# Three layers in split precision: when sums of weights are asked for, which engine makes their low words, and where a plain pair of blocks stands

## The chip, the cores and the metric

The kernel runs on one core of a Trainium2 chip. A core has TensorE (matrix products, PE in the rows, with PEld for its loads of the stationary operand), VectorE (DVE), ScalarE (ACT), GpSimd (POOL) and SyncE (SP, which only issues transfers here). The metric is the device time of one execution in microseconds (us), lower is better. Products accumulate in PSUM banks; all other tiles lie in SBUF. GpSimd reads and writes SBUF only in this kernel.

## The reference, cut to what matters

Attention with a window and block summaries comes first (batch 2, 8 heads, 768 positions, 64 per head); its output is a matrix x of 1536 tokens by 512. Then:

```
h = np.maximum(np.maximum(x @ w1, x @ w2), x @ w3)   # 512 -> 768, layer 1
y = h @ w_out                                        # 768 -> 512, layer 2
out = (y @ w_a) * (y @ w_b) @ w_out2                 # 512 -> 1536 -> 512, layers 3 and 4
```

The diff touches layer 1 for the second half of the tokens.

## The kernel before, in words

**Precision.** A float32 operand is kept as two parts: a high word (ScalarE copies it to the rounded type) and a low word (the operand minus the high word). A product of two operands is three matmuls: high by high, low by high, high by low (`mm3`, L532). `w_parts` (L464, L465) makes the two words of a weight, `split` (L536, L537) those of an activation `hg`; the low word's engine is an argument of both.

**Tokens and blocks.** The tokens are four chunks of 384 columns, c = 0 to 3. Layer 1 has six output blocks f, each with three weights m (w1, w2, w3) of which the maximum is taken. Chunks 0 and 1 are done by `layers12` while the attention of chunks 2 and 3 still runs. Chunks 2 and 3 are done together by `pair1`, the function of the diff.

**Plain and fast pairs.** `pair1` takes two blocks f and f+1 with the same m as a 2x2 matrix problem: two blocks by two chunks. The order of these nine pairs is (0,0), (0,1), (0,2), (2,0), and so on to (4,2), where the first number is f and the second is m. A plain pair (`plain`) is 4 steps of 12 matmuls 128x384. A fast pair needs 7 products instead of 8 (`products`, table PRODUCTS): 7 steps of 6 matmuls, since a product of the table covers half of the contraction. `products` takes two fast pairs in turn, u = 0 and 1, so one turn has 14 steps. Products 0, 3 and 6 need the weights as they are; products 1, 2, 4 and 5 need sums of weights (S1 to S4), and most need sums of x (T1 to T4, made by `x_sums`).

**Sums of weights.** `w_sums` (from L609) makes them for one pair: GpSimd adds high and low words back to float32 (`rc`, two instructions 128x512, L614), VectorE makes four sums 128x256 (`s`, L471 to L474), ScalarE makes two high words (`wt<-s`, L464), and VectorE two low words (`wt<-s`, L465). Their buffers are the tag `ws`, of which WS are allowed. They are asked for at the steps WSUMS among the plain pairs, and within `products` behind products 2 and 5 of u = 1.

**Results.** `result` takes a finished product to float32 `pt` (ScalarE L638 for the first m of a plain pair, VectorE L640 or L633 and L635 for the others, which also take the maximum). When three values of m are seen, `split` makes the block's `hg`: ScalarE its high word, GpSimd its low word (VectorE for the last two blocks of chunk 3).

**Order.** The order of instructions on each engine is set when the program is built, from the dependencies and a timeline that the scheduler computes; TensorE may so run products of a later step first. Two things bind it by hand: `flush` delays the results of a step until the next step's matmuls are written, and `behind_marks` puts what is written in it behind the last marked instruction of its own engine: `mark[0]` on VectorE, `mark[1]` on ScalarE, `mark[2]` on GpSimd (the last `split` there).

**What surrounds it.** `layer2` multiplies the six `hg` of a chunk with w_out (`py`), 72 matmuls for a chunk; it comes after all pairs for chunks 2 and 3. At each step of `pair1` the loop at the end calls `weights(1)`, which brings weights of layers 3 and 4: SyncE issues the load (L434), ScalarE and VectorE take the 64-bit words apart (L454, L456, L458, L459), GpSimd adds the two halves (`w<-w`, int32, L460), then sums and words as above. `fits` lets them on only while no more than ROOM places are held beyond those freed (`w_freed`), and the first three of these loads wait for a small copy of a finished `hg` (`gate`, L433). SUMS names the steps at which sums of y for chunks 0 and 1 (batch 0) are made (`sums_of`, L742 to L747).

Of the kernel before, what the change touches and what calls it, by code (L numbers as in the profile page):

```python
# [19 lines left out]
P = 128  # L20
# [16 lines left out]
NCH, MAXT = len(CHUNKS), max(SIZES)  # L37
# [5 lines left out]
N1, N2, NK = 3 * FF1 // P, FF1 // P, FF2 // P // 3  # L43
# [9 lines left out]

W64, W32, WBUFS, QB, FB, SM, GB, BANKS = (6, 3), (4, 3), (24, 10), 4, (8, 1), 2, (12, 9), (2, 2, 1, 2, 2)

GATE, ROOM, SUMS, EARLY34 = (2, 1), 14, (40, 44, 48, 52), 6
PLAIN, XSUMS, WSUMS, WS, PT, MAX_G, LO_G = 3, (3, 5), (8, 10), 7, 7, False, False
RING, LEAD, TURN, ERA0, ASKS, AHEAD, PRE, TURNS = 8, 5, (11, 2, 4), 8, (3, 4, 5, 7, 9), (4, 1), 3, ((6, N1 - 6, 6, 4, 4), (24, 34), (34, 43))

# [10 lines left out]
def attention_then_maxout_then_bilinear(ctx: ExitStack, tc: tile.TileContext, qt, kt, vt, vwin, wall, const, out):  # L78
# [66 lines left out]
    @contextmanager  # L145
    def behind_marks():

        with ExitStack() as pins:
            for ins in mark + [marks.get(("normal", len(groups) - 1))]:
                if ins is not None:  # L150
                    pins.enter_context(tc.issue_after(ins))
            yield
# [362 lines left out]
    def flush():  # L515
        while late:
            late.pop(0)()

    def bank(name):

        return ps_m.tile([P, 512], F32, tag="m", name=name)

    def ring(name):
        return ps_m.tile([P, 512], F32, tag="r", name=name, bufs=RING)[:, 0:MAXT * P]
# [4 lines left out]
    def mm3(ps, w, o, x, first, last, more=False):  # L529

        for n, (i, j) in enumerate(((0, 0), (1, 0), (0, 1))):
            ins = T.matmul(ps, w[:, i, o:o + P], x[:, j], start=first and n == 0, stop=last and n == 2, skip_group_check=more).ins  # L532
        return ins

    def split(dst, src, eng):
        A.activation(dst[:, 0], src, AF.Copy)  # L536
        ins = eng.tensor_tensor(dst[:, 1], src, dst[:, 0], ALU.subtract).ins  # L537
        if eng is G:
            mark[2] = ins
# [44 lines left out]
    def x_sums(k):  # L584

        if not xs:
            both_x = x_p.tile([P, 4, 2, 2, MAXT * P], F32R, tag="xs", name="xs", bufs=1)
            xs.update({f"T{j + 1}": both_x[:, j] for j in range(4)})

        def whole(c, k):  # L590
            t = y_p.tile([P, MAXT * P], F32, tag="xr", name="xr", bufs=4)
            G.tensor_tensor(t, x_t[c, k][:, 0], x_t[c, k][:, 1], ALU.add)
            return t

        def diff(name, x, y):
            t = y_p.tile([P, MAXT * P], F32, tag="xd" + name, name="xd", bufs=1)
            V.tensor_tensor(t, x, y, ALU.subtract)
            A.activation(xs[name][:, 0, k], t, AF.Copy)
            V.tensor_tensor(xs[name][:, 1, k], t, xs[name][:, 0, k], ALU.subtract)
            return t  # L600

        b11, b12 = whole(2, k), whole(3, k)
        t1 = diff("T1", b12, b11)
        b22, b21 = whole(3, 2 + k), whole(2, 2 + k)
        t2 = diff("T2", b22, t1)
        diff("T3", b22, b12)
        diff("T4", b21, t2)

    def w_sums(f, m):  # L609

        w0, w1 = (w_t[3 * (f + i) + m] for i in range(2))
        r0, r1 = (w32_p.tile([P, 512], F32, tag="rc", name="rc", bufs=2) for _ in range(2))
        for r, w in ((r0, w0), (r1, w1)):
            G.tensor_tensor(r, w[:, 0], w[:, 1], ALU.add)  # L614
        s12, s34 = sums4(*(r[:, o:o + 256] for r in (r0, r1) for o in (0, 256)))
        eng = G if LO_G else V
        s12, s34 = (w_parts(x, eng, "ws") for x in (s12, s34))
        w_s[f, m] = {"A11": (w0, 0), "A12": (w0, 256), "A22": (w1, 256),
                     "S1": (s12, 0), "S2": (s12, 256), "S3": (s34, 0), "S4": (s34, 256)}
# [3 lines left out]
    def pair1():  # L623

        nonlocal w_freed
        part, seen, hs = {}, {}, {2: {}, 3: {}}

        def result(f, c, to, x=None):

            prev, t = part.get((f, c)), half("pt")  # L630
            part[f, c] = t
            if x is not None:
                mark[0] = V.tensor_tensor(t, to, x, ALU.add).ins  # L633
                if prev is not None:
                    ins = (G if MAX_G else V).tensor_tensor(t, t, prev, ALU.max).ins  # L635
                    mark[2 if MAX_G else 0] = ins
            elif prev is None:
                mark[1] = A.activation(t, to, AF.Copy).ins  # L638
            else:
                mark[0] = V.tensor_tensor(t, to, prev, ALU.max).ins  # L640
            seen[f, c] = seen.get((f, c), 0) + 1
            if seen[f, c] == 3:
                hs[c][f] = h = hg_p.tile([P, 2, MAXT * P], F32R, tag="hg", name="hg")
                split(h, t, V if f >= N2 - 2 and c == 3 else G)
                if c == GATE[0] and f == GATE[1]:
                    gate.append(h[:, 0, 0:1])

        def plain(f, m):

            nonlocal w_freed  # L650
            for c in (2, 3):
                for i in range(2):
                    ps = bank("ph")[:, 0:MAXT * P]
                    for k in range(4):
                        mm3(ps, w_t[3 * (f + i) + m], k * P, x_t[c, k], k == 0, k == 3)
                    flush()
                    late.append(lambda f=f + i, c=c, ps=ps: result(f, c, ps))
                    yield
            w_freed += 2

        def operand(name, k):
            if name in xs:
                return xs[name][:, :, k]
            return x_t[1 + int(name[2]), 2 * (int(name[1]) - 1) + k]

        def products(two, ahead):

            nonlocal w_freed
            ps, kept = {}, {}
            for i in range(7):  # L670
                for u, (f, m) in enumerate(two):
                    w, y, name = PRODUCTS[i]
                    first = (u, name) not in ps
                    if first:
                        ps[u, name] = ring(f"h{name}")
                    (wt, o), to = w_s[f, m][w], ps[u, name]
                    for k in range(2):
                        mm3(to, wt, o + k * P, operand(y, k), first and k == 0, k == 1, not first)
                    flush()

                    def evac(i=i, u=u, f=f, to=to):
                        if i < 3:
                            kept[u, i] = t = half(("s1", "m5", "u2")[i])
                            mark[1] = A.activation(t, to, AF.Copy).ins
                        elif i == 3:
                            result(f, 2, to, kept[u, 0])
                        elif i == 4:
                            result(f + 1, 3, to, kept[u, 1])
                        elif i == 5:
                            result(f, 3, to, kept[u, 2])  # L690
                        else:
                            result(f + 1, 2, to)

                    late.append(evac)
                    if (i, u) in ((2, 1), (5, 1)) and ahead:
                        with behind_marks():
                            w_sums(*ahead.pop(0))
                    yield
            w_freed += 2 * len(two)

        order = [(f, m) for f in range(0, N2, 2) for m in range(3)]
        fast = order[PLAIN:]
        ahead, step = fast[:], 0
        for f, m in order[:PLAIN]:
            for _ in plain(f, m):
                step += 1
                with behind_marks():
                    if step in XSUMS:
                        x_sums(XSUMS.index(step))
                    elif step in WSUMS:  # L710
                        w_sums(*ahead.pop(0))
                yield
        while len(fast) - len(ahead) < 2:
            with behind_marks():
                w_sums(*ahead.pop(0))
        for j in range(0, len(fast), 2):
            yield from products(fast[j:j + 2], ahead)
        for c in (2, 3):
            yield from layer2(c, hs[c], ring)
        w_freed += N2  # L720
# [43 lines left out]
    def half(tag):  # L764
        return mo_p.tile([P, MAXT * P], F32, tag=tag, name=tag, bufs={"ca": 9, "t": 3, "pt": PT}.get(tag, 2))
# [138 lines left out]
    for i, _ in enumerate(pair1()):  # L904
        with behind_marks():
            weights(1)
            if i in SUMS:
                m = SUMS.index(i)
# [60 lines left out]
```

## Time and profile before

| | before |
|---|---|
| median of three runs | 562.57 us (562.47 to 563.86) |
| the profiled execution | 563.56 us, its span 561.8 us |
| TensorE busy | 539.5 us (96% of the span) |
| VectorE busy | 422.7 us (75%) |
| ScalarE busy | 283.1 us (50%) |
| GpSimd busy | 237.9 us (42%) |
| mean granted TensorE clock | 0.991 |

Durations in the rows are those of the profiled execution, and times count from the start of its span; 1.76 us of its time lie outside the span. The granted clock is given as a share of 2.4 GHz. `x12` is a count of instructions, `out<-in` names the tiles. Where a row ends in brackets, the engine sat idle before it for that time, and the arrow names what ended the idle time. Idle time of an engine costs nothing by itself: it counts where TensorE, which has the most work, waits at the end of the chain.

### The profile page before, as it was taken

The numbers are of one execution on the slowest core, as the hardware profiler recorded it, in microseconds if no ns is written. First come the engines' busy times: TensorE is split into PE (matmuls) and PEld (weight loads), VectorE is DVE, ScalarE is ACT, GpSimd is POOL, SyncE is SP. The second block draws the span as 40 slices with busy tenths as digits, with TensorE's granted clock in tenths as the row PEclk, the third lists the DMA queues.
The fourth block names the chain that finished last, engine by engine and source line by source line (L and its number), as shares of the span: only waits on it lengthen the run. The fifth ranks groups of instructions, "written<-read, shape, count | busy, mean of one in ns | idle before, by whom it ended". The sixth has DMA issues, their size and how long they took to land.

```text
span 561.8 us, 9048 instructions
## 1 busy us (share of the span) xinstructions
PE 539.5 (96%) x3328; PEld 510.8 (91%) x3328; DVE 422.7 (75%) x875; ACT 283.1 (50%) x692; POOL 237.9 (42%) x195
## 2 busy tenths in 40 slices
PE   7899999999999999797999899999999999999997
PEld 7789999999999999796999878988998998998986
DVE  4798976875445569589899898797797798584464
ACT  4699765766533334364866553544552653340130
POOL 3479997642144263544426523521441252140130
PEclk9999999999999999889999999999999999999999
DMA  8994534383000000131131232222123111000015
GB/s 302 359 299 163 190 114 146 120 272 108 22 1 2 1 0 1 56 129 48 70 112 49 104 113 82 69 76 75 39 76 113 39 50 63 0 1 2 0 39 187
DMA packets 17132, 51.82 MB, mean 92 GB/s; under 512 B 2112, under 2 KB 2752, under 8 KB 17088
## 3 DMA queue, kind: packets, MB, share of 16 engines
q1 hardware_dynamic: 17088, 51.25, 27.2%
q8 instruction: 26, 0.43, 0.3%
q14 instruction: 18, 0.15, 0.1%
HBM read 48.09 MB, written 3.15 MB: 91 GB/s over the span
## 4 chain that ended last, share of the span: by engine, by line
PE 74%; DVE 14%; POOL 4%; ACT 3%; DMA 2%; issue 1%; SPq 1%; POOLq 0%; ACTq 0%; DVEq 0%
PE ph L532 18%; PE qb L532 12%; PE py L532 8%; PE qg L532 6%; PE po L841 5%; PE po L840 5%; PE po L842 5%; PE qd L532 3%; PE ps L261 3%; PE hb L532 3%; DVE wt L465 3%; PE psv L318 2%; POOL w L460 2%; PE pst L299 2%; DVE w L459 1%
## 5 line engine op out<-in xcount | busy, mean ns | idle before, releaser
L460 POOL TENSOR_TENSOR w<-w,w 128x512 int32<-128x512 int32 x60 | 94.0, 1573 | 137.1 <-DVE w L459 84.6
L532 PE MATMUL qb<-yt,wt 128*128 128x384 f32 x576 | 109.3, 335 | 0.3 <-ACT s L791 0.3
L532 PE MATMUL ph<-x,wt 128*128 128x384 f32 x576 | 106.8, 339 | 0.0
L532 PEld LDWEIGHTS qb<-yt,wt 128*128 128x128 f32 x576 | 100.9, 188 | 1.6 <-ACT s L791 0.6
L532 PEld LDWEIGHTS ph<-x,wt 128*128 128x128 f32 x576 | 99.2, 188 | 0.3
L808 POOL TENSOR_TENSOR t<-t,ca 128x384 f32<-128x384 f32 x36 | 44.0, 1236 | 68.9 <-DVE t L807 68.8
L532 PE MATMUL py<-hg,wt 128*128 128x384 f32 x288 | 56.6, 347 | 4.1 <-ACT hg L536 4.1
L532 PE MATMUL qg<-yt,wt 128*128 128x384 f32 x288 | 57.5, 335 | 1.0 <-DVE acc L852 1.0
L842 PE MATMUL po<-wt,hg 128*128 128x512 f32 (+1 forms) x146 | 56.7, 388 | 1.5 <-DVE hg L537 1.5
L840 PE MATMUL po<-wt,hg 128*128 128x512 f32 (+1 forms) x146 | 57.0, 390 | 0.1
L854 DVE TENSOR_TENSOR acc<-po,acc 128x512 f32<-128x512 f32 (+1 forms) x61 | 40.7, 680 | 21.3 <-PE po L842 21.2
L841 PE MATMUL po<-wt,hg 128*128 128x512 f32 (+1 forms) x146 | 56.6, 388 | 0.0
L532 PEld LDWEIGHTS py<-hg,wt 128*128 128x128 f32 x288 | 51.5, 195 | 4.6 <-ACT hg L536 4.4
L532 PEld LDWEIGHTS qg<-yt,wt 128*128 128x128 f32 x288 | 50.5, 188 | 1.3 <-DVE acc L852 1.3
L536 ACT ACTIVATE hg<-t 128x384 fp32r<-128x384 f32 x60 | 30.5, 520 | 37.0 <-POOL t L808 32.1
L268 ACT ACTIVATE s<-s,nm 128x120 f32<-128x120 f32 x96 | 36.9, 386 | 21.5 <-DVE nm L267 21.3
L454 ACT ACTIVATE w<-w 128x512 f32<-128x512 f32 x30 | 20.3, 677 | 48.6 <-DMA w<-wall 48.5
L464 ACT ACTIVATE wt<-w 128x512 fp32r<-128x512 f32 (+1 forms) x60 | 34.7, 583 | 13.1 <-POOL w L460 12.9
L456 ACT ACTIVATE w<-w 128x512 int32<-128x512 uint32 x60 | 39.3, 668 | 3.4 <-DMA w<-wall 3.3
L286 POOL TENSOR_TENSOR s<-s,r 128x720 f32<-128x720 f32 x16 | 22.3, 1391 | 42.6 <-DVE r L284 35.7
L465 DVE TENSOR_TENSOR wt<-w,wt 128x512 fp32r<-128x512 f32 (+1 forms) x44 | 36.3, 824 | 4.8 <-ACT wt L464 4.8
L537 DVE TENSOR_TENSOR hg<-t,hg 128x384 fp32r<-128x384 f32 x48 | 35.2, 740 | 4.2 <-ACT hg L536 4.1
(114 smaller groups left out, 977.6 us busy)
## 6 DMA issues: line engine op xcount, KB each, us to landing
w<-wall SPq DMA_DIRECT2D x60, 512.0 KB, 3.7
qv<-qt SPq DMA_DIRECT2D x15, 384.0 KB, 7.1
row<-kt SPq DMA_DIRECT2D x8, 416.0 KB, 3.6
full<-vt SPq DMA_DIRECT2D x8, 384.0 KB, 7.3
out<-acc SPq DMA_DIRECT2D x11, 256.0 KB, 2.0
qv<-vwin SPq DMA_DIRECT2D x12, 192.0 KB, 5.5
qv<-vwin SPq DMA_DIRECT2D x12, 96.0 KB, 5.3
qv<-qt SPq DMA_DIRECT2D x1, 256.0 KB, 5.4
```

The source lines that it names most:

```text
L268: A.activation(s[:, a], s[:, a], AF.Exp, bias=nm[:, a:a + 1], scale=-1.0, accum_out=sm[:, a:a + 1])
L456: A.activation(lw.bitcast(I32), lw, AF.Copy, scale=2.0 ** -29)
L460: G.tensor_tensor(w.bitcast(I32), w.bitcast(I32), lw.bitcast(I32), ALU.add)
L464: A.activation(w[:, 0], r, AF.Copy)
L465: eng.tensor_tensor(w[:, 1], r, w[:, 0], ALU.subtract)
L532: ins = T.matmul(ps, w[:, i, o:o + P], x[:, j], start=first and n == 0, stop=last and n == 2, skip_group_check=more).ins
L537: ins = eng.tensor_tensor(dst[:, 1], src, dst[:, 0], ALU.subtract).ins
L808: G.tensor_tensor(t, t, cs[c, f], ALU.mult)
L840: T.matmul(ps, g[:, 0], w[:, 0], start=(f == 0), stop=False)
L841: T.matmul(ps, g[:, 0], w[:, 1], start=False, stop=False)
L842: ins = T.matmul(ps, g[:, 1], w[:, 0], start=False, stop=(f == 1)).ins
L854: V.tensor_tensor(acc[c, i][:, cols_], ps, acc[c, i][:, cols_], ALU.add)
```

## The change

The number of plain pairs at the front falls from three to two, and the last pair (4,2) becomes plain and stands behind the fast ones. It takes its PSUM banks from the ring of eight that the fast pairs use; the plain pairs at the front use two banks as before. The six fast pairs are (0,2) to (4,1). Within `products` the sums of weights for the next turn are asked for behind products 0 and 2 of u = 1. The low words of these sums are made by GpSimd (LO_G). The steps of XSUMS, WSUMS and SUMS are smaller, WS is 8 instead of 7, and ROOM 16 instead of 14. ERA0 (buffers of the first weights) and FB (buffers of the rows of keys and values of batch 0) are larger by two and one.

```
-W64, W32, WBUFS, QB, FB, SM, GB, BANKS = (6, 3), (4, 3), (24, 10), 4, (8, 1), 2, (12, 9), (2, 2, 1, 2, 2)
+W64, W32, WBUFS, QB, FB, SM, GB, BANKS = (6, 3), (4, 3), (24, 10), 4, (9, 1), 2, (12, 9), (2, 2, 1, 2, 2)
...
-GATE, ROOM, SUMS, EARLY34 = (2, 1), 14, (40, 44, 48, 52), 6
-PLAIN, XSUMS, WSUMS, WS, PT, MAX_G, LO_G = 3, (3, 5), (8, 10), 7, 7, False, False
-RING, LEAD, TURN, ERA0, ... = 8, 5, (11, 2, 4), 8, ...
+GATE, ROOM, SUMS, EARLY34 = (2, 1), 16, (40, 43, 46, 49), 6
+PLAIN, XSUMS, WSUMS, WS, PT, MAX_G, LO_G, ASK = (2, 1), (2, 4), (5, 7), 8, 7, False, True, (0, 2)
+RING, LEAD, TURN, ERA0, ... = 8, 5, (11, 2, 4), 10, ...
...
-        def plain(f, m):
+        def plain(f, m, bank):
...
-                    ps = bank("ph")[:, 0:MAXT * P]
+                    ps = bank("ph")
...
-                    if (i, u) in ((2, 1), (5, 1)) and ahead:
+                    if u == 1 and i in ASK and ahead:
...
-        fast = order[PLAIN:]
+        fast = order[PLAIN[0]:len(order) - PLAIN[1]]
         ahead, step = fast[:], 0
-        for f, m in order[:PLAIN]:
-            for _ in plain(f, m):
+        for f, m in order[:PLAIN[0]]:
+            for _ in plain(f, m, lambda name: bank(name)[:, 0:MAXT * P]):
...
         for j in range(0, len(fast), 2):
             yield from products(fast[j:j + 2], ahead)
+        for f, m in order[len(order) - PLAIN[1]:]:
+            yield from plain(f, m, ring)
```

## Rows read from the trace of the kernel before

**Rows 1.** Waits of TensorE: us in total, times, longest us.

```profile
PE hg L532 <- ACT wt L464: 4.4, 2, 3.7
PE py L532 <- ACT hg L536: 4.1, 1, 4.1
```

**Rows 2.** TensorE's timeline: start us, us, instruction, idle time before it.

```profile
217.19 0.44 PE L532 MATMUL hg<-xs,wt 128*128 128x384 f32 x1 [0.75 <-ACT wt L464]
...
236.77 0.69 PE L532 MATMUL hg<-xs,wt 128*128 128x384 f32 x1 [3.69 <-ACT wt L464]
...
266.48 12.09 PE L532 MATMUL py<-hg,wt 128*128 128x384 f32 x60 [4.06 <-ACT hg L536]
```

**Rows 3.** Windows: stretch, length, busy of PE, PEld, DVE, ACT, POOL; clock, DMA, GB/s.

```profile
217.20:233.00 15.80, 15.80 (x90) 15.56 (x90) 10.36 (x21) 7.61 (x16) 5.09 (x5) 1.00 0.00 0
233.00:236.80 3.80, 0.11 (x2) 0.03 (x1) 3.53 (x6) 0.71 (x2) 3.10 (x5) 0.82 0.06 17
236.80:243.40 6.60, 6.60 (x24) 6.60 (x25) 4.71 (x9) 3.60 (x6) 0.00 (x0) 0.59 0.62 230
243.40:262.40 19.00, 19.00 (x110) 18.70 (x108) 18.36 (x31) 10.59 (x19) 8.80 (x5) 1.00 0.25 84
262.40:266.50 4.10, 0.04 (x2) 0.03 (x1) 3.53 (x7) 0.91 (x3) 3.16 (x1) 0.96 0.00 0
266.50:278.40 11.90, 11.90 (x60) 11.90 (x61) 10.39 (x15) 10.46 (x20) 4.42 (x3) 0.87 0.27 90
...
320.00:340.00 20.00, 18.39 (x80) 14.44 (x80) 20.00 (x37) 9.24 (x17) 4.12 (x5) 1.00 0.39 142
340.00:366.00 26.00, 24.12 (x135) 23.07 (x134) 20.57 (x34) 13.10 (x28) 12.27 (x10) 1.00 0.16 53
```

**Rows 4.** Chain that ended last: start us, us, piece.

```profile
217.81 2.08 PE hd L532 x12
...
236.77 0.69 PE hg L532
237.46 0.32 PE hb L532
237.78 3.84 PE hd L532 x12
241.62 1.90 PE py L532 x9
...
259.91 5.66 POOL w L460
...
266.48 12.09 PE py L532 x60
```

**Rows 5.** GpSimd's timeline in the stage.

```profile
193.73 1.02 POOL L537 TENSOR_TENSOR hg<-pt,hg 128x384 fp32r<-128x384 f32 x1 [18.35 <-ACT hg L536]
...
229.93 1.02 POOL L537 TENSOR_TENSOR hg<-pt,hg 128x384 fp32r<-128x384 f32 x1 [3.70 <-ACT hg L536]
230.91 2.53 POOL L614 TENSOR_TENSOR rc<-wt 128x512 f32<-128x512 f32 x2
...
235.05 1.05 POOL L433 COPY w<-hg 128x1 f32<-128x1 f32 x3
```

**Rows 6.** Durations in ns (min/median/max): line 465 on VectorE and GpSimd, line 614.

```profile
L465 DVE TENSOR_TENSOR wt<-s,wt x12: 678/685/1777, 190.9 to 237.4; 128x512 fp32r<-128x512 f32 x12
...
L465 POOL TENSOR_TENSOR wt<-w,wt x16: 1267/1294/1741, 34.5 to 104.9; 128x512 fp32r<-128x512 f32 x16
...
L614 POOL TENSOR_TENSOR rc<-wt x12: 1285/1292/1747, 165.0 to 232.2; 128x512 f32<-128x512 f32 x12
```

**Rows 7.** Timelines of SyncE and VectorE: layer 3's first weights.

```profile
235.46 62.47 SPq L434 DMA_DIRECT2D w<-wall  x12
...
240.80 0.68 DVE L458 TENSOR_SCALAR w<-psw 128x512 uint32<-128x512 uint32 x1
```

**Rows 8.** Windows: the opening.

```profile
0.00:30.00 30.00, 24.00 (x219) 21.97 (x220) 19.18 (x77) 16.81 (x66) 11.86 (x26) 1.00 0.95 324
```

More of the change, by code (lines that the diff above doesn't have):

```diff
@@ L52 @@
             ("S4", "B22", "g"), ("A22", "T4", "b"))
-W64, W32, WBUFS, QB, FB, SM, GB, BANKS = (6, 3), (4, 3), (24, 10), 4, (8, 1), 2, (12, 9), (2, 2, 1, 2, 2)
-GATE, ROOM, SUMS, EARLY34 = (2, 1), 14, (40, 44, 48, 52), 6
-PLAIN, XSUMS, WSUMS, WS, PT, MAX_G, LO_G = 3, (3, 5), (8, 10), 7, 7, False, False
-RING, LEAD, TURN, ERA0, ASKS, AHEAD, PRE, TURNS = 8, 5, (11, 2, 4), 8, (3, 4, 5, 7, 9), (4, 1), 3, ((6, N1 - 6, 6, 4, 4), (24, 34), (34, 43))
+W64, W32, WBUFS, QB, FB, SM, GB, BANKS = (6, 3), (4, 3), (24, 10), 4, (9, 1), 2, (12, 9), (2, 2, 1, 2, 2)
+GATE, ROOM, SUMS, EARLY34 = (2, 1), 16, (40, 43, 46, 49), 6
+PLAIN, XSUMS, WSUMS, WS, PT, MAX_G, LO_G, ASK = (2, 1), (2, 4), (5, 7), 8, 7, False, True, (0, 2)
+RING, LEAD, TURN, ERA0, ASKS, AHEAD, PRE, TURNS = 8, 5, (11, 2, 4), 10, (3, 4, 5, 7, 9), (4, 1), 3, ((6, N1 - 6, 6, 4, 4), (24, 34), (34, 43))
 EARLY, BIAS_DVE, SPLIT_DVE = 16, ((0, 1, 0), (0, 1, 0), (0, 0, 0)), ((0, 0, 1), (0, 0, 1), (1, 1, 1))
```

## The prediction

> **What bounds the kernel now.** I read the table of busy times first: TensorE is the bound, busy 96% of the span, so the change can win only where TensorE idles or runs at a lower clock. The waits of TensorE say where that is [rows 1]: the two largest entries, 4.4 us behind ScalarE's `wt` (line 464) and 4.1 us behind ScalarE's `hg` (line 536), both stand in `pair1`, the stage that the diff touches. TensorE's timeline dates them [rows 2]: 0.75 us before 217.19, 3.69 us before 236.77, 4.06 us before 266.48. The windows show what follows each [rows 3]: in the 3.8 us of the second wait the granted clock falls to 0.82, and in the 6.6 us behind it the mean is 0.59, that is, mostly the 1.2 GHz level; behind the third it is 0.87 for 11.9 us. The stretch behind the short first wait keeps 1.00. So a wait of 0.75 us costs itself, one of about 4 us costs a slow stretch too.
>
> The chain that ended last prices the slow stretches [rows 4]. Twelve matmuls 128x384 took 2.08 us at full clock, 0.1733 us each. After the second wait 1, 1, 12 and 9 took 0.69 + 0.32 + 3.84 + 1.90 = 6.75 us where 23 x 0.1733 = 3.99 were due: 2.76 us lost. After the third, 60 took 12.09 us where 10.40 were due: 1.69 us lost.
>
> Why the waits? The second one: the sums of weights for the last pair to be multiplied are asked for at product 5 of the pair before, and GpSimd's part is pinned behind the last split traced until then. Its timeline shows just this [rows 5]: a split `hg` at 229.93, then the two `rc` at once from 230.91, after GpSimd had idled 3.70 us. Then come four sums on VectorE and ScalarE's high word, and TensorE starts at 236.77 [rows 2]. The third wait has another cause: GpSimd's add at line 460, for a weight of layer 3, took 5.66 us from 259.91 [rows 4], with VectorE busy 18.36 of the 19.0 us before and 3.53 of the 4.1 us of the wait [rows 3]. ScalarE stood in line behind it and then made `hg`, which layer 2 needs. TensorE had by then done all of layer 2 that did not hang on it.
>
> **The change part by part.** *Asks at products 0 and 2 instead of 2 and 5 (ASK).* A product step is 6 matmuls, 1.04 us, and a pair of fast blocks is two such steps per product, so the second ask moves by 3 x 2 x 1.04 = 6.2 us and the first by 4.2 us. More important is the pin: in the new order the two pairs of blocks that finish a split in one turn of `products` do so from product 3 on, so at product 2 the last split traced is one of the turn before. The last sums then stand behind nothing newer. From the ask to the use (product 1 of the next pair, second block) there are five steps now, 5.2 us, and will be eleven, 11.4 us, against a chain of 236.77 - 230.91 = 5.86 us [rows 2, 5]. So the first two waits go whole: 0.75 + 3.69 + 2.76 = 7.20 us.
>
> *Low words on GpSimd (LO_G).* Twelve subtractions 128x512 leave VectorE, at a median of 0.685 us, 8.2 us in all, and cost GpSimd 1.294 us each by the 16 of the same line that it does early in the kernel, 15.5 us in all [rows 6]. They are on the path only by what they delay: two in a row add 2 x (1.294 - 0.685) = 1.2 us to a chain that now has 4 us of room. GpSimd's load per turn of two pairs: 4 `rc` x 1.292 + 4 low words x 1.294 = 10.3 us and four splits of about 1.02, 14.4 us, against 84 matmuls x 0.1733 = 14.6 us of TensorE. That is tight, but the sums for the first turn run ahead of it: GpSimd idled 18.35 us before 193.73 [rows 5], and the second `rc` is no longer pinned behind a split of the plain pairs. Behind the low words there wait on GpSimd the next `rc` and the splits, which layer 2 needs late only.
>
> *One plain pair less in front, one at the end (PLAIN, XSUMS, WSUMS, `ring`).* Count and price of matmuls stay (12 per plain step, 2.08 us). In front, 4 x 2.08 = 8.3 us of cover are lost for the sums of x and the first two sums of weights, which are asked for one and three steps sooner; the seven products of the first pair, which need the first sums alone, give 7.3 us to cover the second. At the end the last `hg` of chunk 2 comes 4.2 us before the plain steps end, and with layer 2 on the other five blocks 15 x 0.1733 = 2.6 us more lie ahead; all of layer 2 on blocks 0 to 3, 96 matmuls or 16.6 us, hangs on nothing late. ScalarE was 4.06 us late, so I take the third wait as gone: 4.06 + 1.69 = 5.75 us. If the order of TensorE doesn't use that cover, all of it stays.
>
> *Edits costed at nothing.* WS 8 gives the sums asked sooner a place; without it they would wait for the turn before to end, at worst the old 3.69. SUMS moves the sums of y for batch 0 along with the stage. ROOM 16 against 14 makes up for fewer places freed by then (12 instead of 14 at the start of the third turn), so layer-3 weights open there in both; only at the end are two more places open. Their issue on SP's queue stood at 235.46, VectorE's first step for them at 240.80 [rows 7], late because the gate's copies stood on GpSimd behind the late `rc`, at 235.05 [rows 5]; I expect both some 14 us sooner. ERA0 and FB touch loads of the opening, where TensorE is 24.0 of 30 us busy and DMA at 0.95 [rows 8]: two more early buffers ask nothing sooner there; bounds 1 us either way, from that idle 6 us.
>
> *New waits, not in this trace.* There are three places (the second sums in the first turn, GpSimd in the second, the last `hg` in layer 2). Below: nothing. Above: one like that before 236.77 with its slow stretch, 6.45 us [rows 2, 4]. The nearest row is the short one, 0.75 us, since a chain that starts six steps sooner misses by little; three make 2.25. *Layer 3 and 4:* TensorE idled 1.61 us in 320 to 340 and 1.88 in 340 to 366, with VectorE at 20.0 of 20 and 20.57 of 26 [rows 3]. VectorE has 8.2 us less to do, but TensorE comes some 11 sooner. I take zero, between -3.49 and +7.06 (VectorE's work that lies inside the two long waits now, 3.53 + 3.53).
>
> **The sum.** 7.20 + 5.75 - 2.25 = 10.7 us. The profiled execution took 563.56 (span 561.8 and 1.76 around it), which gives 552.9; it lies 0.99 above the median of the three runs, 562.57, against which the forecast is **551.9 us**.
>
> **The rivals.** *The third wait stays.* GpSimd's slow add needs only dense VectorE work, and that is still there. For it: 5.66 us for an operation on 128x512 where 1.3 is usual [rows 6]. Against it: the plain steps' cover. Time: 551.9 + 5.75 - 0.75 (its allowance) = 556.9. Chance 0.18.
>
> *VectorE takes it back in layer 3.* TensorE arrives earlier and finds the same queue of weights: up to 7.06 us come back, 559.0; with more, it ends near no change. Against it: the weights start earlier and VectorE was 10.36 of 15.8 us busy before 233 [rows 3], room to fill. Chance 0.12.
>
> *GpSimd becomes the bound, and the kernel is slower.* With each of the eight `rc` and low words of a turn at the slowest row, 1.747, and the splits 1.7 times slower too, a turn takes 14.0 + 7.0 = 21 us against 14.6: 6.4 us late, in the second and third turns, each with a slow stretch of 2.76. Then 562.57 - 12.95 + 2 x 9.2 = 568. It decides from about 1.65 us for the mean of an `rc` or low word, where the 4 us of room are eaten. For: the one add of 5.66 us; against: the median of the twelve `rc` is 1.292 [rows 6], beside a VectorE that was then busier than it will be. Chance 0.11. The Trainium skill (GPSIMD Engine Reference, Key points) states a rule for this rival: GpSimd shares its SBUF interfaces with VectorE and contends with Vector instructions that have two SBUF inputs. By that rule nearly each of the new low words would meet one, and the time would be the 568 above; the trace agrees in the 5.66 us row, but not in the median of 1.292.
>
> *The change does not do what it says.* Each sum is still pinned to the last VectorE and ScalarE instruction of the stage, so asking sooner might move nothing on these queues; then only the third wait goes: 556.8. Chance 0.06.
>
> **How the numbers follow.** The forecast has 0.48, the rivals 0.18, 0.12, 0.11 and 0.06, and 0.05 is left for an order of TensorE or a place in memory that I cannot see. A measurement of this kernel tells 0.3%, 1.7 us, from no change. The forecast, the first and fourth rival and two thirds of the second are faster: 0.80. A third of the second and some of the rest is the same: 0.06. GpSimd's rival and the rest is slower: 0.14. The low end is the forecast without new waits and with most of the 3.49 us of layers 3 and 4: 562.57 - 12.95 - 3.1 = 546.5. The high end takes in the first, most of the second and the fourth rival: 559.5. That holds 0.48 + 0.18 + 0.10 + 0.06 = 0.82.
>
> **What would show it.** Right: no TensorE wait on `wt` of line 464 in `pair1`; `rc` of the last sums at least 8 us before their first matmul; low words `wt<-s` on GpSimd near 1.3 us; granted clock 1.00 through the stage; layer 3 starting about 11 us sooner; the first issue of layer-3 weights near 221. Wrong: a wait of 3 us or more anywhere in `pair1` with its slow stretch, above all on GpSimd's `wt`; an add of line 460 over 5 us with TensorE waiting on `hg` behind it; or larger TensorE waits on VectorE between the start of layer 3 and 60 us on.

## The result, and the profile after

The changed kernel takes 549.81 us in the median of four runs (549.45 to 551.07), the kernel before 563.22 in four: a ratio of 0.9763, with a 95% interval of 0.9736 to 0.979. The forecast was 551.9. The profiled execution after took 549.45 us with a span of 547.2.

To see where the time went I cut each trace at two rows of TensorE's timeline, which stand for the end of the opening with the first half of the tokens (the first `ph` of a plain pair of chunks 2 and 3) and the start of layer 3 (the first `qb`). Before:

```profile
172.06 4.47 PE L532 MATMUL ph<-x,wt 128*128 128x384 f32 x24
...
278.40 1.20 PE L532 MATMUL qb<-yt,wt 128*128 128x384 f32 x6
```

After:

```profile
170.90 4.43 PE L532 MATMUL ph<-x,wt 128*128 128x384 f32 x24
...
266.96 1.20 PE L532 MATMUL qb<-yt,wt 128*128 128x384 f32 x6
```

So the first part shrank from 172.06 to 170.90 us, the stage between (the function of the diff and layer 2 behind it, "the stage" from here) from 106.34 to 96.06, and layers 3 and 4 from 561.8 - 278.40 = 283.40 to 547.2 - 266.96 = 280.24: 1.16 + 10.28 + 3.16 = 14.60 us of span. (The time of the profiled execution fell by 14.11, since 2.25 us lie outside the span after and 1.76 before.) The windows of the whole stage, before and after (columns as in [rows 3]):

```profile
172.06:278.40 106.34, 97.85 (x540) 96.89 (x537) 79.81 (x136) 50.29 (x98) 41.98 (x32) 0.95 0.12 40
```

```profile
170.90:266.96 96.06, 94.30 (x540) 92.86 (x537) 79.63 (x128) 51.27 (x100) 56.45 (x44) 1.00 0.14 50
```

The matmuls are 540 in both. TensorE idled 8.49 us before and 1.76 after, and was busy 97.85 and 94.30: 6.73 us of the 10.28 are idle time, 3.55 are slow stretches at a lower clock.

TensorE's timeline after, at the places that answer to [rows 2], with the idle time before each instruction in brackets:

```profile
216.15 1.33 PE L532 MATMUL hb<-xs,wt 128*128 128x384 f32 x6 [0.25 <-DVE pt L633]
...
221.73 0.44 PE L532 MATMUL hg<-xs,wt 128*128 128x384 f32 x1 [0.40 <-ACT wt L464]
...
243.95 23.17 PE L532 MATMUL py<-hg,wt 128*128 128x384 f32 x132 [1.06 <-DVE pt L640]
```

The waits of 0.75 and 3.69 us on `wt` have become one of 0.40; another of 0.25 us is on VectorE's `pt`. The one of 4.06 us before layer 2 is 1.06 and no longer on `hg`: TensorE waits for VectorE's `pt` (L640). The windows of the changed kernel show the clock:

```profile
204.00:220.00 16.00, 15.70 (x89) 15.02 (x88) 10.91 (x17) 5.40 (x12) 12.21 (x11) 1.00 0.00 1
220.00:236.00 16.00, 15.60 (x90) 15.16 (x89) 11.36 (x19) 9.59 (x18) 8.31 (x10) 1.00 0.28 99
236.00:252.00 16.00, 14.94 (x86) 14.62 (x85) 16.00 (x26) 10.24 (x19) 7.01 (x4) 1.00 0.38 133
252.00:268.00 16.00, 16.00 (x94) 16.00 (x93) 15.31 (x26) 11.56 (x23) 6.41 (x3) 1.00 0.19 67
...
310.00:330.00 20.00, 20.00 (x94) 17.07 (x93) 19.85 (x37) 8.91 (x16) 5.59 (x4) 1.00 0.34 128
330.00:356.00 26.00, 26.00 (x152) 26.00 (x151) 22.61 (x37) 15.06 (x32) 11.17 (x9) 1.00 0.11 42
```

The granted clock is 1.00 throughout, where [rows 3] has 0.59 and 0.87. From 236 to 268 VectorE is as full as it was, 16.00 and 15.31 of 16 us. The waits of 320 to 366 in [rows 3] are gone too: TensorE is busy for all of 310 to 356. GpSimd's timeline from the second half of the second turn on, for [rows 5]:

```profile
206.50 3.77 POOL L614 TENSOR_TENSOR rc<-wt 128x512 f32<-128x512 f32 x3
...
213.73 1.47 POOL L614 TENSOR_TENSOR rc<-wt 128x512 f32<-128x512 f32 x1
...
216.72 1.33 POOL L537 TENSOR_TENSOR hg<-pt,hg 128x384 fp32r<-128x384 f32 x1
...
221.75 1.56 POOL L465 TENSOR_TENSOR wt<-s,wt 128x512 fp32r<-128x512 f32 x1 [1.02 <-ACT wt L464]
...
226.44 1.16 POOL L433 COPY w<-hg 128x1 f32<-128x1 f32 x3
```

The last `rc` now come before, not behind, the splits of blocks 2 and 3, of which the first is at 216.72; the last of them starts 8.0 us before the matmul at 221.73 that needs them. Of these 8.0 us VectorE's queue takes a part: that `rc` ends at 215.20, and the first of VectorE's four sums starts at 218.04, behind results of the pairs before (VectorE's timeline of the changed kernel):

```profile
217.58 0.54 DVE L633 TENSOR_TENSOR pt<-hg,u 128x384 f32<-128x384 f32 x1
218.04 0.41 DVE L471 TENSOR_TENSOR s<-rc 128x256 f32<-128x256 f32 x1
```

The low words run on GpSimd, and the gate's copies stand at 226.44. The durations, for [rows 6], and SyncE's first issue for layer 3, for [rows 7]:

```profile
L465 POOL TENSOR_TENSOR wt<-s,wt x12: 1283/1329/1622, 182.0 to 224.2; 128x512 fp32r<-128x512 f32 x12
...
L614 POOL TENSOR_TENSOR rc<-wt x12: 1277/1290/1597, 163.8 to 213.7; 128x512 f32<-128x512 f32 x12
```

```profile
227.40 60.16 SPq L434 DMA_DIRECT2D w<-wall  x14
```

### The profile page after: what moved, and what is told of

It is laid out like the page before. It is cut to its first block, busy times and chain, and to the rows that moved or that the text cites. A ratio compares the mean times of both kernels' runs of the same rounds, so it can differ in the third digit from the quotient of the medians.

```text
span 547.2 us, 9042 instructions
## 1 busy us (share of the span) xinstructions
PE 534.0 (98%) x3328; PEld 506.3 (93%) x3328; DVE 422.2 (77%) x863; ACT 284.6 (52%) x692; POOL 245.9 (45%) x207
## 4 chain that ended last, share of the span: by engine, by line
PE 80%; DVE 9%; POOL 4%; issue 2%; ACT 1%; DMA 1%; DVEq 0%; POOLq 0%; ACTq 0%
PE ph L532 17%; PE qb L532 16%; PE py L532 9%; PE qg L532 8%; PE po L843 6%; PE po L844 6%; PE po L842 6%; PE qd L532 4%; PE ps L261 3%; PE psv L318 2%; PE pst L299 2%; POOL wt L465 1%; DVE yt L745 1%; DVE yd L749 1%; DVE w L459 1%
## 5 line engine op out<-in xcount | busy, mean ns | idle before, releaser
L460 POOL TENSOR_TENSOR w<-w,w 128x512 int32<-128x512 int32 x60 | 85.3, 1431 | 140.5 <-DVE w L459 79.9
L532 PE MATMUL py<-hg,wt 128*128 128x384 f32 x288 | 54.0, 340 | 1.1 <-DVE pt L640 1.1
L532 PEld LDWEIGHTS py<-hg,wt 128*128 128x128 f32 x288 | 49.5, 188 | 1.6 <-DVE pt L640 1.4
L465 DVE TENSOR_TENSOR wt<-w,wt 128x512 fp32r<-128x512 f32 (+1 forms) x44 | 33.7, 768 | 1.5 <-ACT wt L464 1.3
```

The costliest lines, as they stand in the source:

```text
L460: G.tensor_tensor(w.bitcast(I32), w.bitcast(I32), lw.bitcast(I32), ALU.add)
L465: eng.tensor_tensor(w[:, 1], r, w[:, 0], ALU.subtract)
```

## The experiments

Each kernel was made from the one before or the changed one by the edits shown, and timed beside the kernel before. Every change of a number also moves tiles in SBUF and the order that the scheduler writes, so one part's worth is not read from the total alone; the table cuts the one profiled execution of each kernel at the two rows named above.

| kernel | median us | ratio to before (95%) | opening | stage | layers 3, 4 |
|---|---|---|---|---|---|
| before | 563.22 | | 172.06 | 106.34 | 283.40 |
| changed | 549.81 | 0.9763 (0.9736 to 0.979) | 170.90 | 96.06 | 280.24 |
| before_plain_end | 564.77 | 1.0033 (1.0008 to 1.0058) | 175.81 | 104.00 | 284.49 |
| before_ask | 557.51 | 0.9911 (0.9882 to 0.9941) | 170.79 | 98.63 | 285.68 |
| before_low_words | 569.92 | 1.0114 (1.0066 to 1.0162) | 175.71 | 113.15 | 280.04 |
| after_low_words_back | 556.39 | 0.991 (0.988 to 0.994) | 170.45 | 101.49 | 283.86 |
| after_plain_front | 560.68 | 0.9975 (0.9961 to 0.9988) | 170.90 | 103.25 | 284.35 |
| after_opening_back | 551.93 | 0.9819 (0.9789 to 0.9849) | 175.07 | 96.13 | 281.10 |
| after_ask_back | 563.12 | 1.0012 (0.9999 to 1.0025) | 171.19 | 107.42 | 282.69 |
| after_room_back | 554.60 | 0.9857 (0.9843 to 0.9872) | 171.01 | 95.44 | 285.45 |
| after_third_low_words | 559.63 | 0.9941 (0.9923 to 0.9959) | 171.59 | 96.12 | 291.79 |
| after_back_and_third | 564.45 | 1.0037 (1.0015 to 1.0058) | 170.78 | 100.03 | 290.89 |
| after_again | 549.71 | 0.9778 (0.9756 to 0.98) | 170.57 | 95.97 | 280.86 |
| after_half_low_words | 554.08 | 0.9839 (0.9818 to 0.986) | 171.11 | 97.37 | 284.12 |

**The plain pair at the end, alone.**

```
-PLAIN, XSUMS, WSUMS = 3, (3, 5), (8, 10)
+PLAIN, XSUMS, WSUMS = (2, 1), (2, 4), (5, 7)
```

> The kernel before with the order of pairs alone changed: two plain pairs in front, pair (4,2) plain at the end, XSUMS (2,4), WSUMS (5,7). Asks stay at products 2 and 5, low words stay on VectorE. My theory: the wait of 4.06 us of TensorE on hg before layer 2 and its slow stretch go (5.75 us), the waits on wt of line 464 stay, so about 557 us, some 1% below before. Rival (GpSimd's add starved by VectorE decides, not the cover): the wait on hg stays, 562 to 564 us.

It is no faster. The wait before layer 2 is gone, as my theory says, but the two on `wt` grew from 0.75 and 3.69 us to these (TensorE's timeline of this kernel):

```profile
214.93 0.45 PE L532 MATMUL hg<-xs,wt 128*128 128x384 f32 x1 [2.11 <-ACT wt L464]
...
236.00 0.69 PE L532 MATMUL hg<-xs,wt 128*128 128x384 f32 x1 [6.20 <-ACT wt L464]
```

The stage gained 2.34 us in place of 5.75. The opening of the profiled execution was 3.75 us longer than before, with ERA0 and FB unchanged, and that execution (566.12) lies above the median; so the loss is not the stage's. That pair's worth depends on when the sums are asked for.

**The early asks, alone.**

```
-if (i, u) in ((2, 1), (5, 1)) and ahead:
+if u == 1 and i in (0, 2) and ahead:
-WS 7, ERA0 8, FB (8, 1)
+WS 8, ERA0 10, FB (9, 1)
```

> The kernel before with the asks at products 0 and 2 and WS 8 (with the buffers ERA0 10 and FB 9); low words stay on VectorE, three plain pairs in front. My theory: both waits on wt of line 464 go with the slow stretch, 7.20 us, the wait on hg before layer 2 stays, so about 556 us. Rival (the pins of VectorE and ScalarE hold the sums where they were): the wait of 3.69 us stays, 562 to 564 us. If VectorE takes the gain back in layers 3 and 4: the waits go but the time from the start of layer 3 to the end grows by several us.

The time is near my number, but not for my reason alone. TensorE's timeline of this kernel:

```profile
215.37 1.76 PE L532 MATMUL hb<-xs,wt 128*128 128x384 f32 x6 [2.36 <-DVE pt L633]
217.36 0.69 PE L532 MATMUL hg<-xs,wt 128*128 128x384 f32 x1 [0.22 <-ACT wt L464]
...
256.63 12.96 PE L532 MATMUL py<-hg,wt 128*128 128x384 f32 x70 [0.25 <-DVE pt L640]
```

The waits on `wt` fall to 0.22 us; one of 2.36 us on VectorE's `pt` is new. And the wait before layer 2 goes as well, to 0.25 us, though no plain pair stands at the end: GpSimd's slow add, from which I had that wait, does not come up, since no add of line 460 in this kernel takes more than 2.62 us. The stage gains 7.71 us, and layers 3 and 4 give 2.28 of it back: the rival that has VectorE take it back shows itself here.

**The low words on GpSimd, alone.**

```
-LO_G = False
+LO_G = True
```

> The kernel before with the low words of the sums on GpSimd alone. My theory: by itself this makes the chain of the last sums longer by 1.2 us and frees 8.2 us of VectorE, so the wait before the last pair grows to about 5 us and the time is 563 to 566 us. Rival (VectorE is the bound behind the waits): the time falls by 2 us or more, to 561 or less.

It is slower by more than either expected. The wait before the last pair is 7.18 us, and VectorE's `pt` was late for another of 4.39 (TensorE's timeline, then GpSimd's):

```profile
222.05 0.44 PE L532 MATMUL hg<-xs,wt 128*128 128x384 f32 x1 [2.02 <-ACT wt L464]
...
246.71 0.69 PE L532 MATMUL hg<-xs,wt 128*128 128x384 f32 x1 [7.18 <-ACT wt L464]
...
265.84 2.29 PE L532 MATMUL hb<-xs,wt 128*128 128x384 f32 x6 [4.39 <-DVE pt L633]
```

```profile
240.23 1.35 POOL L537 TENSOR_TENSOR hg<-pt,hg 128x384 fp32r<-128x384 f32 x1 [6.66 <-ACT hg L536]
241.55 2.47 POOL L614 TENSOR_TENSOR rc<-wt 128x512 f32<-128x512 f32 x2
```

The late `rc` are still pinned behind a split, so the chain only grew. The stage lost 6.81 us; the opening of this execution was 3.65 us longer, and layers 3 and 4, at 280.04 us, 3.36 shorter than before.

**The low words back on VectorE, in the changed kernel.**

```
-LO_G = True
+LO_G = False
```

> The changed kernel with the low words back on VectorE. My theory: with the early asks there is room, so no wait of over 1 us comes back in layer 1, and the time stays within 1 us of the changed kernel's 549.8. Rival (the 3.2 us that layers 3 and 4 gained come from VectorE's 8.2 us less work): 552 to 554 us, with the waits of layer 3 back. Second rival (VectorE too dense in the second and third turn): a wait on wt of 2 us or more.

My theory falls: 6.6 us are lost, 5.43 in the stage and 3.62 in layers 3 and 4, while the opening is 0.45 shorter and the profiled execution, 557.59, lies above the median. The two windows from 236 to 252 (this kernel; the changed one's stands above) and TensorE's rows in this kernel:

```profile
236.00:252.00 16.00, 13.37 (x66) 12.92 (x66) 16.00 (x24) 9.62 (x17) 4.26 (x3) 0.89 0.25 88
```

```profile
185.75 0.44 PE L532 MATMUL hg<-xs,wt 128*128 128x384 f32 x1 [1.16 <-ACT wt L464]
...
247.36 24.74 PE L532 MATMUL py<-hg,wt 128*128 128x384 f32 x132 [2.53 <-DVE pt L640]
...
281.02 1.74 PE L532 MATMUL qb<-yt,wt 128*128 128x384 f32 x8 [2.68 <-ACT y L728]
```

VectorE is full in both, but here TensorE waits 2.53 us for it at 247.36 in place of 1.06, and the 132 matmuls behind that take 24.74 us in place of 23.17, at a clock of 0.89 in the window. In the whole stage VectorE is 88.97 us busy here, 79.63 in the changed kernel. So the low words matter here mostly by VectorE's backlog at the end of the stage; of the waits that came back, 1.16 us at 185.75 and 0.41 at 186.78 (on VectorE's low word itself) are on the sums.

**Half of the low words.** S1 and S2, which are needed first, on VectorE, the others on GpSimd:

```
-s12, s34 = (w_parts(x, eng, "ws") for x in (s12, s34))
+s12, s34 = (w_parts(x, e, "ws") for x, e in ((s12, V), (s34, eng)))
```

> The changed kernel with the low words of S1 and S2 on VectorE and those of S3 and S4 on GpSimd. Theory (VectorE's load in the stage costs, roughly in step with what it gets back): half of the 6.6 us between all on VectorE and all on GpSimd, 552 to 554 us. Rival (the sooner-needed half was late on GpSimd, and sharing is best): 548 to 549 us, without the wait of 0.4 us on wt.

554.08 is a little beyond the upper end of the first theory and speaks against the rival. Not all of it is in step: the stage loses 1.31 us of the 5.43 that it loses with all of them back, but layers 3 and 4 lose 3.88, as much as with all (3.62). The wait before layer 2 is 1.46 us, between 1.06 and 2.53, and one on VectorE's `ca` in layer 3 is 2.33 (1.3 in the changed kernel):

```profile
245.48 23.17 PE L532 MATMUL py<-hg,wt 128*128 128x384 f32 x132 [1.46 <-DVE pt L640]
...
289.95 2.11 PE L532 MATMUL qb<-yt,wt 128*128 128x384 f32 x6 [2.33 <-DVE ca L803]
```

**More of it: a third of the low words of layers 3 and 4 on GpSimd**, in the changed kernel and in the one with the low words of layer 1 back on VectorE:

```
-SPLIT_DVE = ((0, 0, 1), (0, 0, 1), (1, 1, 1))
+SPLIT_DVE = ((0, 0, 1), (0, 0, 1), (1, 1, 0))
```

> The changed kernel with a third of the low words of layers 3 and 4 on GpSimd too (each third weight; up to now all on VectorE). Theory: VectorE's density before and in layer 3 is what is left to gain, so the waits of TensorE on VectorE around the start of layer 3 (1.3 and 0.5 us) and before layer 2 (1.1 us) shrink: 547 to 549 us. Rival (GpSimd is now in the chain of those weights): new waits on wt, 551 to 556 us.

> The changed kernel with the low words of layer 1's sums back on VectorE, as in an earlier run that took 556.4 us, and each third low word of layers 3 and 4 on GpSimd instead. Theory (VectorE's load before layer 3 counts, not which instruction leaves it): part of the 6.6 us comes back, 551 to 554 us. Rival (the low words of layer 1 themselves were late on VectorE): 556 us or more, with the wait of 2.5 us before layer 2 unchanged.

The theory fails in both: the stage keeps its length in the first (96.12) and is 1.46 us shorter in the second (100.03 against 101.49), but layers 3 and 4 become 11.6 and 7.0 us longer. In the first of the two kernels, GpSimd's timeline, the durations of line 465 there, and the window around these two:

```profile
273.69 6.98 POOL L465 TENSOR_TENSOR wt<-s,wt 128x512 fp32r<-128x512 f32 x2 [2.77 <-ACT wt L464]
```

```profile
L465 POOL TENSOR_TENSOR wt<-s,wt x22: 1288/1592/5297, 182.7 to 457.2; 128x512 fp32r<-128x512 f32 x22
```

```profile
273.00:281.00 8.00, 6.57 (x33) 5.60 (x33) 8.00 (x14) 6.33 (x15) 7.31 (x3) 1.00 0.13 46
```

Two low words took 6.98 us, the first of them 5.30 (the longest of the 22), with VectorE 8.00 of 8.00 us busy, where the median in the changed kernel's stage is 1.329. The same move that helps where VectorE has gaps (10.91 and 11.36 of 16 us busy in the windows from 204 to 236) hurt where it was full; how much of the 11.6 us comes from such low words was not traced.

**The plain pair back in front, and the opening's numbers as before.**

```
-PLAIN, XSUMS, WSUMS = (2, 1), (2, 4), (5, 7)
+PLAIN, XSUMS, WSUMS = (3, 0), (3, 5), (8, 10)
-ERA0 10, FB (9, 1)
+ERA0 8, FB (8, 1)
```

> The changed kernel with all three plain pairs in front again (XSUMS (3,5), WSUMS (8,10)) and the opening's buffers as before (ERA0 8, FB 8). If the plain pair at the end is what removes the wait on hg before layer 2, that wait of about 4 us and its slow stretch come back: 555 us. Rival, from the run of the early asks alone, which had no such wait: it stays away, and layer 1 and 2 of the second half take about 96 to 98 us, so the time is within 2 us of the changed kernel's 549.8 apart from what the opening costs.

> The changed kernel with ERA0 8 and FB 8 as before; the control of the run above. My theory: the opening's edits ask nothing sooner, so the time stays within 1 us of 549.8. Rival: these two numbers decide where tiles lie in SBUF, and loads of the opening then wait for other tiles; TensorE loses 2 to 4 us before 120 us and the time is 552 to 554 us.

The stage loses 7.1 us against the control's 96.13. No wait on `hg` is back; the time goes in several waits of 0.3 to 1.9 us (TensorE's waits of this kernel, two largest of the stage):

```profile
PE hg L532 <- ACT wt L464: 3.0, 2, 1.9
PE hb L532 <- DVE pt L633: 2.3, 2, 1.5
```

This edit does not take the plain pair alone: with three pairs in front and ROOM 16 the loads of layer 3 start at 205.81 us instead of 227.40, and two adds of line 460 (217.45 and 220.54) stand on GpSimd among the `rc` and low words of the last sums. So the 7.1 us are the pair's place and these weights together.

The control itself is 2.1 us slower than the changed kernel in the median. Its profiled execution, the slowest of the four (554.47; the two fastest took 550.78 and 550.94), has the opening at 175.07 us, with a wait of 2.0 us on VectorE's `kept` (1.1 in the changed kernel) and one on a load that the changed kernel has not,

```profile
PE ps L261 <- DVE kept L179: 2.0, 1, 2.0
...
PE ps L261 <- DMA qv<-qt: 1.7, 1, 1.7
```

In the table the kernels with ERA0 10 and FB 9 have openings of 170.45 to 171.59 us, those with 8 and 8 of 170.90 to 175.81. After_again repeats the changed kernel:

> The changed kernel once more, as the measure for the runs beside it. All theories: 549 to 551 us; its opening, up to the first plain pair, is 170.9 us long as before if the 1.2 us gained there belong to the change, and 172 us or more if they are scatter of single executions.

Its opening is 170.57 us. That the old numbers leave the opening to scatter and the new ones do not is a pattern over kernels with one traced execution each, not shown for one kernel; which tile's place would decide it was not tried.

**The asks back, and ROOM as its control.**

```
-ASK = (0, 2), ROOM 16
+ASK = (2, 5), ROOM 14
```

```
-ROOM 16
+ROOM 14
```

> The changed kernel with the asks back at products 2 and 5, and ROOM 14. My theory: the waits on wt of line 464 come back, longer than before since the low words on GpSimd lengthen the chain: about 2 and 7 us with slow stretches, 561 to 564 us. Rival (the plain pair at the end and GpSimd's share make the ask's place unimportant): 550 to 552 us.

> The changed kernel with ROOM 14; the control of the run above. With 14 the first weights of layer 3 open only when 14 places are freed, a turn later. My theory: VectorE, which is near full before layer 3, then starts them some 14 us later and TensorE waits in layer 3: 552 to 556 us. Rival: the weights were early enough, 549 to 551 us.

With the asks and ROOM back all of the gain is gone. The control has a stage of 95.44 us, this one 107.42: 12.0 us by the asks alone. In the medians they are worth 8.5 (563.12 against 554.60), since layers 3 and 4 are 2.76 us shorter here. The waits (TensorE's timeline of the kernel with the asks back, then GpSimd's):

```profile
212.45 0.69 PE L532 MATMUL hg<-xs,wt 128*128 128x384 f32 x1 [4.22 <-ACT wt L464]
...
235.41 0.69 PE L532 MATMUL hg<-xs,wt 128*128 128x384 f32 x1 [5.50 <-ACT wt L464]
```

```profile
228.21 1.02 POOL L537 TENSOR_TENSOR hg<-pt,hg 128x384 fp32r<-128x384 f32 x1 [3.83 <-ACT hg L536]
229.19 2.80 POOL L614 TENSOR_TENSOR rc<-wt 128x512 f32<-128x512 f32 x2
...
235.43 2.52 POOL L465 TENSOR_TENSOR wt<-s,wt 128x512 fp32r<-128x512 f32 x2 [0.58 <-ACT wt L464]
```

As in [rows 5], the last `rc` start the moment the split before them ends, and the matmul follows 6.2 us later. The low words begin when the wait is over, so they are no part of it.

ROOM alone costs 4.8 us, and all of it behind the stage: layers 3 and 4 take 5.2 us more. My reason for it was wrong, since layer 3's first issue is at 227.46 in this kernel too. What differs is the start of layer 3 (first this kernel, then the changed one):

```profile
267.00:285.00 18.00, 15.36 (x76) 14.21 (x75) 16.78 (x31) 12.65 (x28) 5.56 (x4) 0.91 0.08 30
...
267.00:285.00 18.00, 16.32 (x91) 15.33 (x89) 16.79 (x32) 12.31 (x26) 4.85 (x4) 1.00 0.28 87
```

In these 18 us DMA moved 30 GB/s here and 87 there, TensorE was busy 15.36 against 16.32 us, and its clock fell to 0.91. It did 15 matmuls less, 2.6 us of the 5.2 at 0.1733 each.

## Why the prediction was right, and where it was not

The time and the sign are right, by the mechanism of the forecast in its main term. Point by point:

*The first two waits.* Right: 7.20 us were to go, and 0.40 us on `wt` and 0.25 on `pt` are left. The run with the asks back puts 12.0 us of the stage on this part, more than I did; with the other parts in place the old asks make longer waits (4.22 and 5.50). The rival that the pins hold everything fell with it. But the 4 us of room that I gave the chain were not there: it took 8.0 us from its last `rc` instead of 5.86, with the sums behind VectorE's queue. I overlooked that queue in the kernel before too: there a sum of y (`yt`, L743, 1.90 us from 232.35) holds VectorE's first sum until 234.18, 0.74 us behind the end of the `rc`.

*The third wait.* Right in size (1.06 us is left, within the 2.25 allowed for new waits), wrong in cause. I gave it to the plain pair at the end. The early asks alone removed it as well, in a kernel without an add of line 460 over 2.62 us, and the plain pair alone removed it but made the first two longer, so that little was won. Slow adds are still there in the changed kernel (4.02 us the longest), without a wait of TensorE on `hg` behind one. Without the plain pair at the end its stage is 7.1 us longer, with small waits on the sums and on VectorE, but the earlier weights of layer 3 are in that number; what the pair's place is worth by itself stays open.

*The low words.* Wrong: I costed them at nothing but 1.2 us on a chain with room. Alone they made the stage 6.8 us longer; in the whole they are worth 6.6 us of the time, and the waits that come back without them are mostly on VectorE before layer 2 and on ScalarE's `y` in layer 3. Nor do 8.2 us leave VectorE against the kernel before: it is busy 422.2 us of the span, where it was 422.7 (79.63 and 79.81 in the stage), because other instructions of it take longer. Its twelve maxima of line 635 take 8.9 us in all instead of 6.6, the longest 1.645, where none was over 0.559 before. Against the kernel with the low words back (88.97 in the stage) it does get 9.3.

*GpSimd as the bound.* It did not come: the mean of an `rc` is 1.37 us and of a low word 1.42 (medians 1.290 and 1.329), below the 1.65 from which I had it decide. The Trainium skill (GPSIMD Engine Reference, Key points) states that GpSimd shares its SBUF interfaces with VectorE, in contention with VectorE's instructions of two SBUF inputs. By the medians of this stage that cost GpSimd little; the 5.30 us of a low word where VectorE was full, with such instructions for the most part, agree with it.

*Layers 3 and 4.* The step that failed by most is the term that I took as zero between -3.49 and +7.06: it was -3.16. What keeps the gain is ROOM 16, an edit that I costed at nothing, and the low words: with ROOM 14 these layers are 5.2 us longer than in the changed kernel, and with the low words back 3.62. Against the kernel before, ROOM 14 makes the term +2.05 (285.45 against 283.40), within the up to 7.06 of the rival "VectorE takes it back".

*The opening.* Costed at nothing within 1 us either way; it was 1.16 us in the profiled execution, and 2.1 us by the medians of the changed kernel and its control. That was outside the bound, if it is not scatter: with the old numbers one kernel had an opening of 170.90 too.

*The first issue of layer 3.* I expected 221; it is 227.40, 8 us sooner than before and not 14. The gate's copies stand behind the last splits of blocks 2 and 3 on GpSimd. Low words stand among these, but do not decide it: with the low words back on VectorE the issue is at 227.43. With the early asks alone it is at 235.11, with the plain pair alone at 234.94, so it takes both.

The sum by steps: 10.28 in the stage against 10.7 forecast, and 3.16 + 1.16 us from two terms that I had at zero, 14.6 in all. The closeness in the stage is in part luck, as two errors cancel: the slow stretches, which I priced at 2.76 + 1.69 = 4.45 us, gave back 3.55, and 1.76 us of idle time are left where I had allowed 2.25.

Open is why the early asks and the low words together, without the plain pair at the end, make the stage longer (103.25) than the asks alone (98.63). SUMS, ROOM, ERA0 and FB differ between those two as well; the loads of layer 3 start at 205.81 in the first and at 235.11 in the second, which points to ROOM, but no run held it fixed. The order of TensorE and the places of tiles change with each edit. SUMS by itself was not tried.

## What to carry to other kernels

Look at what a late helper is pinned behind in its own engine's queue: asking for work two and three products sooner was worth 12 us of the stage here. How much of that is the queue entry in front of which it now stands, and how much the steps that it gained, was not separated. Parts of such a change do not add up: the low words on GpSimd made the stage 6.8 us longer alone, while in the whole they were worth 6.6 us of the time; the plain pair at the end won 2.3 us of the stage alone, and the kernel without it, with layer 3's weights early, took 8.8 us more (560.68 against 551.93). Work moved from VectorE to GpSimd paid where VectorE had gaps, and a low word took up to four times as long where VectorE was full, so read both engines' windows for the very stage.

## What the runs showed that was not expected

A low word 128x512 on GpSimd takes 1.329 us in the median where VectorE is some 70% busy (10.91 and 11.36 of 16 us) and up to 5.30 us where it is full. The slowing goes both ways: a maximum of line 635 on VectorE, at most 0.559 us before, took 1.65 us from 213.98 in the changed kernel, beside an `rc` on GpSimd from 213.73 to 215.20. A wait of TensorE of 1.06 us left the clock at 1.00, one of 2.53 us was followed by 132 matmuls in 24.74 us instead of 23.17. And in the kernels with other numbers of two buffers (ERA0 10 and FB 9) the traced openings take 170.45 to 171.59 us, in those with the old ones 170.90 to 175.81; that the two numbers decide it is not shown.
